# One-token decoder layer on one core: K and V loaded in four groups of eight heads instead of eight groups of four

## The chip, the cores and the metric

The kernel runs on one core of one Trainium2 chip. The metric is the device time of one launch in microseconds (us); lower is better. Times come in two kinds: the time of a whole launch, of which several were taken, and one launch under the profiler, whose span runs from its first to its last instruction.

## The reference

One decoder layer for one token. A is attention over a cache of 4096 positions with 32 heads of 128 elements, B is a gated MLP. All data is bf16.

```python
def _A_ref(x, k_cache, v_cache, wq, wo):            # x [1,1,640]; caches [1,32,4096,128]
    q = (x @ wq).reshape(B, Sq, Hq, Dh).transpose(0, 2, 1, 3)      # wq [640, 4096]
    scores = jnp.einsum("bhqd,bhkd->bhqk", q, k) * (Dh ** -0.5)
    p = _softmax(scores, axis=-1)
    o = jnp.einsum("bhqk,bhkd->bhqd", p, v)
    return o.transpose(0, 2, 1, 3).reshape(B, Sq, Hq * Dh) @ wo    # wo [4096, 640]

def _B_ref(x, w_gate, w_up, w_down):                # w_gate, w_up [640, 1728]; w_down [1728, 640]
    h = _gelu(x @ w_gate) * (x @ w_up)
    return h @ w_down

h  = x + _A_ref(_layernorm(x), A_k_cache, A_v_cache, A_wq, A_wo)
h2 = h + _B_ref(_layernorm(h), B_w_gate, B_w_up, B_w_down)
```

The two caches together are 67.1 MB, the weights 17.1 MB. Nothing is used twice.

## The kernel before

There is no scheduler: each operation is appended to its engine's list by hand (`V` VectorE, `A` ScalarE, `T` TensorE, `GP` GpSimd, `P.dma("sync", ...)` for the loads), with the earlier operations that it depends on; the lists are emitted in that order with semaphore waits. An engine therefore waits in order: what stands behind a waiting instruction waits too. All large loads are on SP's one queue.

**Buffers.** `slots` are three buffers of 34,560 B a partition. Each load of K or V for four heads (a group G of 0 to 7) fills 32 KB of one: 32 partitions a head, 128 positions a partition, 4 MB in all. `arena` holds wq and then wo. The order of the loads (`order`, L192) is wq, then K and V of groups 0 to 5 in turn, then K6, K7, V6, V7, then wo in two halves, then w_gate, w_up and w_down in pieces. A load into a slot waits for what last read it (`consumed`): for K that is the last product on VectorE, for V the last matmul.

**Scores** (`score_mult`, `score_sum`, L297 to L320). VectorE multiplies a chunk of 32 positions of every partition with the group's q, kept in `qb`, into one of four `prod` buffers (L301). TensorE folds the 128 elements of each position to 16 by eight matmuls with an identity matrix (the first at L311, the others through the helper at L29), and VectorE sums the 16 (L318) into `sc`. A group has four chunks.

**Softmax** (`head_max`, `exp_group`). The maximum over a partition's positions is taken (L323), scaled, made the maximum over a head's 32 partitions by a transpose of 32 by 32 blocks (L324 to L326), and used as the bias of exp on ScalarE (L329), which also sums. Then VectorE spreads the weights into a masked operand `p_bd` (L332), in which each partition's weight stands in its head's column alone.

**V** (`pv_group`, L337). 32 matmuls of 512 columns go four at a time to the four 32-row quarters of `po`, two banks of PSUM. `pick` (L359) masks what belongs together and `pick_sum` (L363 to L370) adds it up, in the last two groups by three additions. `head_sum` (L372) gathers the parts of a head, `normalize` divides, `spread` and `take` turn the result into columns `aP`, and `proj_part` multiplies them with wo. Behind it come the second layernorm, the gate (`glu`, L514), w_up, gelu, and w_down (`down`, L564).

**Order around the change.** VectorE gets, for each group, products and sums with the sum one chunk behind, the previous group's pick, the softmax, and then `p_bd`. V of group 6 is multiplied while K of group 7 is scored; V of group 7 follows its softmax. The last steps wait for weights that come behind the caches on the queue.

Of the kernel before, what the change touches and what calls it, by code (L numbers as in the profile page):

```python
# [11 lines left out]
D = 640  # L12
# [8 lines left out]
NG = 8  # L21
NSLOT = 3
# [88 lines left out]
def bass_sequential_preLN__gqa_block_cached__glu_gated_geglu__decode_kernel(nc, A_x, A_k_cache, A_v_cache, A_wq, A_wo, B_x, B_w_gate, B_w_up, B_w_down, out):  # L111
    sb = lambda name, shape, dt: nc.alloc_sbuf_tensor(name, shape, dt)
    SLOT = 10 * DF
    slots = [sb("slot%d" % i, [128, SLOT], BF16) for i in range(NSLOT)]
    arena = sb("arena", [128, 5 * 4096], BF16)
    prod = sb("prod", [128, 4, 32, DH], BF16)
    qb = sb("qb", [128, NG, DH], BF16)
    sc = sb("sc", [128, 2, 4, 32], FP32)
    mx = sb("mx", [128, NG], FP32)
    mxd = sb("mxd", [128, 2, 32], FP32)  # L120
    nb = sb("nb", [128, NG], FP32)
    p_t = sb("p_t", [128, 2, 128], BF16)
    p_bd = sb("p_bd", [128, 2, 128, 4], BF16)
    x_row = sb("x_row", [1, D], BF16)
    out_row = sb("out_row", [1, D], BF16)
    xx = sb("xx", [128, 10], FP32)
    ln = sb("ln", [128, 8], FP32)
    xlnB = sb("xlnB", [128, 5, 32], BF16)
    hT = sb("hT", [128, 10], FP32)
    hX = sb("hX", [128, 128, 5], FP32)  # L130
    hlnT = sb("hlnT", [128, 5], BF16)
    rz = sb("rz", [16, 2], FP32)
    po_m = sb("po_m", [128, 8, DH], FP32)
    po_r = sb("po_r", [128, 4, DH + 1], FP32)
    m8_t = sb("m8_t", [128, 8, 4, 4], FP32)
    m8 = sb("m8", [128, 8], FP32)
    hs_t = sb("hs_t", [128, 4, 32], FP32)
    hs = sb("hs", [128, 28], FP32)
    hb = sb("hb", [128, 28], FP32)
    aT = sb("aT", [16, 2, 128], BF16)  # L140
    aP = sb("aP", [128, 2, 16], BF16)
    sel = sb("sel", [16, 8, 128], BF16)
    A_hi = sb("A_hi", [128, D], BF16)
    A_lo = sb("A_lo", [128, D], BF16)
    rows = [sb("rows%d" % i, [128, 512], BF16) for i in range(2)]
# [10 lines left out]
    par_t = sb("par_t", [128, 2, 64], BF16)  # L156
    par = sb("par", [128, 2], FP32)
    one_bf = sb("one_bf", [1, 1], BF16)
    ones_f = sb("ones_f", [128, 128], FP32)
    mean_f = sb("mean_f", [128, 128], FP32)  # L160
    ones_b = sb("ones_b", [128, 1024], BF16)
    id_f = sb("id_f", [128, 128], FP32)
    id_b = sb("id_b", [128, 128], BF16)
    eps_t = sb("eps_t", [128, 1], FP32)
    zero_t = sb("zero_t", [128, 1], FP32)
    psum = lambda i, n=1: nc.alloc_psum_tensor("bank%d" % i, [128, 512 * n], FP32)
# [5 lines left out]
    ps_q = [bank[4], bank[7]]  # L172
# [4 lines left out]
    ps_p = bank[7]  # L177

    wo_sb = arena[:, :].rearrange("p (t i n) -> p t i n", t=2, i=16)
    view = lambda n: slots[n % NSLOT][:, 0:128 * DH].rearrange("p (g d) -> p g d", d=DH)  # L180

# [5 lines left out]


    A(lambda e: e.preload_act_table_set("natural_log_exp_and_others"))
    d_x = P.dma("scalar", x_row[:, :], A_x[0, :, :])  # L190
    d_wq = [P.dma("sync", arena[:, :], A_wq[:, :].rearrange("(p c) n -> p (c n)", c=5))]
    order = [(kind, G) for G in range(NG - 2) for kind in "KV"] + [(kind, G) for kind in "KV" for G in (NG - 2, NG - 1)]  # L192
    pos = {t: n for n, t in enumerate(order)}
    landed, consumed = {}, {}
    state = {"next": 0}
    d_wo = {}

    def wo_load(name, t, lo, hi):
        d_wo[name] = P.dma("sync", wo_sb[:, t, lo:hi, :],
                           A_wo[2048 * t:2048 * t + 2048, :].rearrange("(p i) n -> p i n", i=16)[:, lo:hi, :], qd)  # L200

    def issue(upto):
        while state["next"] < min(upto, len(order)):
            n = state["next"]
            kind, g = order[n]
            src = A_k_cache if kind == "K" else A_v_cache
            src = src[0, 4 * g:4 * g + 4, :, :].rearrange("h (p r) d -> (h p) (r d)", p=32)
            dst = slots[n % NSLOT][:, 0:128 * DH]
            landed[n] = P.dma("sync", dst, src, consumed[n - NSLOT] if n >= NSLOT else None)
            state["next"] = n + 1  # L210

    issue(NSLOT)


    c_one = V(lambda e: e.memset(one_bf[:, :], 1.0))
    c_ones = V(lambda e: e.memset(ones_f[:, :], 1.0))
    c_mean = V(lambda e: e.memset(mean_f[:, :], 1.0 / D))
    V(lambda e: e.memset(eps_t[:, :], EPS))
    c_eps = V(lambda e: e.memset(zero_t[:, :], 0.0))
    c_onesb = GP(lambda e: e.memset(ones_b[:, :], 1.0))  # L220
    c_idb = GP(lambda e: e.affine_select(id_b[:, :], ones_b[:, 0:128], pattern=[[1, 128]], compare_op=ALU.is_equal,
                                         fill=0.0, base=0, channel_multiplier=-1), c_onesb)
    c_idf = GP(lambda e: e.affine_select(id_f[:, :], ones_f[:, :], pattern=[[1, 128]], compare_op=ALU.is_equal,
                                         fill=0.0, base=0, channel_multiplier=-1), c_ones)
    c_sel = GP(lambda e: e.affine_select(sel[:, :, :], ones_b[0:16, :].rearrange("p (a b) -> p a b", a=8),
                                         pattern=[[-1, 8], [1, 128]], compare_op=ALU.is_equal,
                                         fill=0.0, base=0, channel_multiplier=-8), c_onesb)
    c_hz = GP(lambda e: e.memset(hs[:, :], 0.0))
    c_hb = GP(lambda e: e.memset(hb[:, :], 0.0))
    c_hb = GP(lambda e: e.affine_select(hb[:, 12:16], ones_f[:, 0:4], pattern=[[-32, 4]], compare_op=ALU.is_ge,  # L230
                                        fill=0.0, base=0, channel_multiplier=1), c_hb, c_ones)
    c_hb = GP(lambda e: e.affine_select(hb[:, 12:16], hb[:, 12:16], pattern=[[32, 4]], compare_op=ALU.is_ge,
                                        fill=0.0, base=31, channel_multiplier=-1), c_hb)
    c_hs = GP(lambda e: e.affine_select(hs_t[:, :, :], ones_f[:, :].rearrange("p (a b) -> p a b", a=4),
                                        pattern=[[-1, 4], [-4, 32]], compare_op=ALU.is_equal,
                                        fill=0.0, base=0, channel_multiplier=1), c_ones)
    c_s4 = GP(lambda e: e.affine_select(sel4[:, :], ones_b[:, 0:4], pattern=[[-32, 4]], compare_op=ALU.is_equal,
                                        fill=0.0, base=0, channel_multiplier=1), c_onesb)
    c_m8 = GP(lambda e: e.affine_select(m8_t[:, :, :, :], ones_f[:, :].rearrange("p (a b c) -> p a b c", a=8, b=4),
                                        pattern=[[-4, 8], [-32, 4], [-1, 4]], compare_op=ALU.is_equal,  # L240
                                        fill=0.0, base=0, channel_multiplier=1), c_ones)
    c_sel2 = GP(lambda e: e.affine_select(sel2[:, :, :], ones_b[0:64, 0:128].rearrange("p (a b) -> p a b", a=64),
                                          pattern=[[1, 64], [0, 2]], compare_op=ALU.is_equal,
                                          fill=0.0, base=0, channel_multiplier=-1), c_onesb)
    c_par = GP(lambda e: e.affine_select(par_t[:, :, :], ones_b[:, 0:128].rearrange("p (a b) -> p a b", a=2),
                                         pattern=[[-1, 2], [-2, 64]], compare_op=ALU.is_equal,
                                         fill=0.0, base=0, channel_multiplier=1), c_onesb)

    c_hs = V(lambda e: e.reduce_sum(hs[:, 12:16], hs_t[:, :, :], axis=AX.X), c_hs, c_hz)
    c_o4 = V(lambda e: e.reduce_max(ones4[:, :], sel4[:, :], axis=AX.X), c_s4)  # L250
    c_m8 = V(lambda e: e.reduce_sum(m8[:, :], m8_t[:, :, :, :].rearrange("p a b c -> p a (b c)"), axis=AX.X), c_m8)

    V(lambda e: e.reduce_sum(par[:, :], par_t[:, :, :], axis=AX.X), c_par)
# [9 lines left out]
    def layernorm(src, ev, out_fn):  # L263
# [8 lines left out]

    xl = layernorm(xx, xc, lambda e: e.tensor_scalar(
        xlnB[:, :, :], xx[:, 0:5].unsqueeze(2).to_broadcast([128, 5, 32]), ln[:, 0:1], ln[:, 4:5],
        ALU.subtract, ALU.mult))


    wq_j = arena[:, :].rearrange("p (c g j d) -> p c j g d", c=5, g=NG, j=4)

    def q_proj(e):  # L280
        for c in range(5):
            for hf in range(2):
                for j in range(4):
                    args = (ps_q[hf][32 * j:32 * j + 32, :], xlnB[:, c, :], wq_j[:, c, j, 4 * hf:4 * hf + 4, :])
                    if hf == 0:
                        i = e.matmul(*args, start=(c == 0), stop=(c == 4))  # L286
                    else:
                        i = matmul_again(nc, *args, c == 0, c == 4, (128, 32), (0, 32 * j))
        return i
    qd = T(q_proj, xl, *d_wq)  # L290
    qa = V(lambda e: e.tensor_copy(qb[:, 0:4, :].rearrange("p g d -> p (g d)"), ps_q[0][:, :]), qd)  # L291
    qc = A(lambda e: e.copy(qb[:, 4:8, :].rearrange("p g d -> p (g d)"), ps_q[1][:, :]), qd)


    folds, reds, exps, pbs, pvs, evs, hds = {}, {}, {}, {}, {}, {}, {}

    def score_mult(s):  # L297
        G, n = s // 4, pos[("K", s // 4)]
        kt = view(n)
        u = s % 4  # L300
        m = V(lambda e: e.tensor_tensor(  # L301
            out=prod[:, s % 4, :, :], in0=kt[:, 32 * u:32 * u + 32, :],
            in1=qb[:, G, :].unsqueeze(1).to_broadcast([128, 32, DH]), op=ALU.mult),
# [109 lines left out]
    def run(todo):  # L413
        while todo:
            todo.pop(0)()
# [200 lines left out]
```

## Time and profile before

| What | Value |
|---|---|
| Time before, median of 3 runs | 202.68 us (202.64 to 204.21) |
| Time of the profiled execution | 202.77 us |
| Its span | 201.5 us |
| Mean granted TensorE clock | 0.816 |
| Bytes read from HBM | 84.23 MB, 418 GB/s over the span |
| Busy: the load queue, of 16 transfer engines | 97.8% |
| Busy: VectorE / TensorE / ScalarE / GpSimd | 68% / 57% / 4% / 3% |

How to read it: in the lines of the profile PE is TensorE, PEld its weight loads, DVE VectorE, ACT ScalarE, POOL GpSimd and SP the engine that issues the loads. `L301` is a line of the kernel. A group's row gives its count, busy time and mean duration in ns, and after the second bar the idle time of the engine before it with what ended that time. Tile names come without their number: `slot` is any of the three buffers, `bank` any bank of PSUM. The span is 1.3 us shorter than the time of the same execution.

### The profile page before, as it was taken

The numbers are of one execution on the slowest core, as the hardware profiler recorded it, in microseconds if no ns is written. First come the engines' busy times: TensorE is split into PE (matmuls) and PEld (weight loads), VectorE is DVE, ScalarE is ACT, GpSimd is POOL, SyncE is SP. The second block draws the span as 40 slices with busy tenths as digits, with TensorE's granted clock in tenths as the row PEclk, the third lists the DMA queues.
The fourth block names the chain that finished last, engine by engine and source line by source line (L and its number), as shares of the span: only waits on it lengthen the run. The fifth ranks groups of instructions, "written<-read, shape, count | busy, mean of one in ns | idle before, by whom it ended". The sixth has DMA issues, their size and how long they took to land.

```text
span 201.5 us, 1482 instructions
## 1 busy us (share of the span) xinstructions
PE 115.2 (57%) x801; PEld 18.2 (9%) x397; DVE 136.3 (68%) x168; ACT 8.9 (4%) x27; POOL 5.1 (3%) x17
## 2 busy tenths in 40 slices
PE   0107058466628693686169717762874099374585
PEld 0101000010001000100010001000100001022323
DVE  1301088639991799699848985996799979853331
ACT  2101000000000000000000000000000000000111
POOL 7200000000000000000000000000000000000000
PEclk9999658969985579799976997996699669878555
DMA  9999999999999999999999999999999999999992
GB/s 342 431 398 455 449 416 416 423 436 462 439 416 423 418 423 455 455 423 416 423 413 442 449 449 423 416 423 429 442 442 442 423 419 407 439 407 439 414 403 94
DMA packets 4185, 84.31 MB, mean 418 GB/s; under 512 B 466, under 2 KB 980, under 8 KB 1492
## 3 DMA queue, kind: packets, MB, share of 16 engines
q1 hardware_dynamic: 4178, 84.23, 97.8%
q8 instruction: 4, 0.07, 0.1%
q14 instruction: 1, 0.01, 0.0%
q10 hardware_dynamic: 2, 0.00, 0.0%
HBM read 84.23 MB, written 0.00 MB: 418 GB/s over the span
## 4 chain that ended last, share of the span: by engine, by line
DMA 52%; DVE 28%; PE 16%; SPq 1%; issue 1%; ACT 0%
DMA slot<-in_A_k_cache_dram 40%; DVE prod L301 18%; DMA slot<-in_B_w_down_dram 13%; PE bank L29 11%; DVE sc L318 5%; DVE po_r L369 3%; PE bank L347 3%; PE bank L311 2%; SPq L60 1%; DVE p_bd L332 1%; DVE mx L323 1%; PE bank L564 0%; DVE mxd L325 0%; DVE mxd L324 0%; DVE nb L326 0%
## 5 line engine op out<-in xcount | busy, mean ns | idle before, releaser
L301 DVE TENSOR_TENSOR prod<-slot,qb 128x4096 bf16<-128x4096 bf16 x32 | 72.4, 2285 | 22.4 <-DMA slot<-in_A_k_cache_dram 22.4
L29 PE MATMUL bank<-prod,id_b 128*128 128x512 bf16 x224 | 60.8, 417 | 0.0
L347 PE MATMUL bank<-slot,p_bd 128*32 128x512 bf16 x128 | 19.0, 583 | 27.3 <-DVE p_bd L332 27.3
L311 PE MATMUL bank<-prod,id_b 128*128 128x512 bf16 x32 | 14.1, 439 | 35.4 <-DVE prod L301 35.4
L318 DVE TENSOR_REDUCE sc<-bank 128x32 f32<-128x512 f32 x32 | 22.0, 687 | 8.4 <-PE bank L29 8.2
L29 PE MATMUL bank<-slot,p_bd 128*32 128x512 bf16 x128 | 18.9, 580 | 0.0
L311 PEld LDWEIGHTS bank<-prod,id_b 128*128 128x128 bf16 x32 | 3.3, 103 | 89.4 <-DVE prod L301 89.2
L369 DVE TENSOR_REDUCE po_r<-po_m 128x128 f32<-128x1024 f32 x6 | 11.2, 1865 | 0.0
L359 DVE TENSOR_TENSOR po_m<-bank,m 128x1024 f32<-128x1024 f32 x8 | 9.7, 1215 | 2.2 <-PE bank L29 2.2
L329 ACT ACTIVATE p_t<-sc,nb 128x128 bf16<-128x128 f32 x8 | 3.2, 401 | 150.9 <-DVE nb L326 150.9
L347 PEld LDWEIGHTS bank<-slot,p_bd 128*32 128x32 bf16 x128 | 4.5, 130 | 54.4 <-DVE p_bd L332 40.0
L291 DVE CAST qb<-bank 128x512 bf16<-128x512 f32 x1 | 0.7, 690 | 9.3 <-PE bank L29 9.3
L286 PE MATMUL bank<-arena,xlnB 128*32 128x512 bf16 x20 | 2.8, 531 | 7.2 <-DMA arena<-in_A_wq_dram 7.2
L332 DVE TENSOR_TENSOR p_bd<-p_t,hb 128x512 bf16<-128x512 bf16 x8 | 5.5, 682 | 1.1 <-ACT p_t L329 1.1
L514 PE MATMUL bank<-slot,hlnT 128*1 128x512 bf16 (+1 forms) x40 | 4.6, 551 | 1.5 <-DVE hlnT L503 1.5
L376 PE MATMUL bank<-po_r,hs 128*16 128x128 f32 x16 | 3.7, 318 | 1.5 <-DVE po_r L367 1.5
L258 PE MATMUL bank<-one_bf,x_row 1*128 1x1 bf16 x5 | 0.4, 177 | 6.7 <-DMA x_row<-in_A_x_dram 6.7
L405 PE MATMUL bank<-arena,aP 128*1 128x320 bf16 x32 | 2.5, 298 | 1.0 <-DMA arena<-in_A_wo_dram 1.0
L564 PE MATMUL bank<-slot,hm 128*1 128x128 bf16 (+2 forms) x57 | 2.8, 323 | 0.1
L29 PE MATMUL bank<-arena,xlnB 128*32 128x512 bf16 x20 | 2.8, 528 | 0.0
L374 PEld LDWEIGHTS bank<-po_r,hb 128*16 128x16 f32 x16 | 2.0, 124 | 6.1 <-issue 5.8
L323 DVE TENSOR_REDUCE mx<-sc 128x1 f32<-128x128 f32 x8 | 2.3, 286 | 0.3
(94 smaller groups left out, 48.9 us busy)
## 6 DMA issues: line engine op xcount, KB each, us to landing
slot<-in_A_k_cache_dram SPq DMA_DIRECT2D x8, 4096.0 KB, 19.4
slot<-in_A_v_cache_dram SPq DMA_DIRECT2D x8, 4096.0 KB, 18.8
arena<-in_A_wq_dram SPq DMA_DIRECT2D x1, 5120.0 KB, 15.2
arena<-in_A_wo_dram SPq DMA_DIRECT2D x2, 2560.0 KB, 27.6
slot<-in_B_w_gate_dram SPq DMA_DIRECT2D x1, 2160.0 KB, 18.5
slot<-in_B_w_up_dram SPq DMA_DIRECT2D x1, 1296.0 KB, 21.1
slot<-in_B_w_down_dram SPq DMA_DIRECT2D x2, 640.0 KB, 24.4
slot<-in_B_w_up_dram SPq DMA_DIRECT2D x1, 864.0 KB, 22.7
```

The costliest lines, as they stand in the source:

```text
L29: return e.add_instruction(mybir.InstMatmult(name=nc.get_next_instruction_name(), engine=e.engine, start_tensor_calc=start, stop_tensor_ca ...
L301: m = V(lambda e: e.tensor_tensor(out=prod[:, s % 4, :, :], in0=kt[:, 32 * u:32 * u + 32, :], in1=qb[:, G, :].unsqueeze(1).to_broadcast([1 ...
L311: i = e.matmul(*args, start=True, stop=False)
L318: reds[s] = V(lambda e: e.reduce_sum(sc[:, (s // 4) % 2, s % 4, :], ps_f[s % 2][:, :].rearrange("p (g d) -> p g d", d=16), axis=AX.X), fol ...
L323: m = V(lambda e: e.reduce_max(mx[:, G:G + 1], sc[:, G % 2, :, :].rearrange("p u g -> p (u g)"), axis=AX.X), reds[4 * G + 3])
L329: exps[G] = A(lambda e: e.activation(p_t[:, G % 2, :], sc[:, G % 2, :, :].rearrange("p u g -> p (u g)"), ACTF.Exp, bias=nb[:, G:G + 1], sc ...
L332: pbs[G] = V(lambda e: e.tensor_tensor(out=p_bd[:, G % 2, :, :], in0=p_t[:, G % 2, :].unsqueeze(2).to_broadcast([128, 128, 4]), in1=hb[:, ...
L347: return e.matmul(*args, start=(c < 4), stop=(c >= 12))
L359: mks[G] = V(lambda e: e.tensor_tensor(out=po_m[:, :, :], in0=po[:, :].rearrange("p (b d) -> p b d", b=8), in1=m8[:, :].unsqueeze(2).to_br ...
L369: evs[G] = V(lambda e: e.reduce_sum(po_r[:, G % 4, 0:DH], po_m[:, :, :].rearrange("p b d -> p d b"), axis=AX.X), mks[G], hds.get(G - 4))
L376: hds[G] = T(lambda e: e.matmul(ps_a[0:16, at:at + DH], hs[:, 12 - 4 * g:28 - 4 * g], po_r[:, g, 0:DH], start=False, stop=(g == 3), skip_g ...
L514: i = e.matmul(po[32 * a:32 * a + 1, 512 * k:512 * k + n], hlnT[:, c:c + 1], w[:, c, 512 * a:512 * a + n], start=(c == 0), stop=(c == 4))
```

## The change

- K and V come in four groups of eight heads: 16 partitions a head, 256 positions a partition, rows of 64 KB, 8 MB a load. The last K alone comes in two halves, each half the positions of every partition. The order is wq, K0, V0, K1, V1, K2, V2, K3 (two halves), V3, wo, MLP weights.
- Three buffers of 64 KB a partition hold everything: buffer 2 first wq and some constants, then K1, V2 and wo; buffer 0 holds K0, V1, K3 and then all MLP weights; buffer 1 holds V0, K2, V3 and later a few small rows. `arena` and `prod` are gone.
- The product is written over K itself. A K buffer is free when the last fold on TensorE has read it, and no longer after the last product on VectorE.
- A group has eight chunks. The pick, head sum and, in group 2, the first normalize, spread and take stand between the chunks of the next group.
- The softmax works on 256 positions a partition. As two heads now share a 32-row block, `far` adds a large number in the other head's columns before the minimum.
- `p_bd` of a group is made in four parts (`PARTS`), each followed by its 16 matmuls on V: 64 of 512 columns a group, each with its own weights, into one bank of PSUM. Before there were 32 matmuls for half as many heads, two to a weight load.
- `pick` works on 512 columns instead of 1024, followed by two additions. `spread` is one matmul instead of eight, `take` a masked product and a sum instead of a copy.
- The identity is loaded on TensorE only where another operand was loaded since.
- The q projection writes one bank by 40 matmuls with masked columns (`xlnM`).

The diff, cut to its core:

```diff
-NG = 8
-NSLOT = 3
+NG = 4
+SLOT = 256 * DH
...
-    order = [(kind, G) for G in range(NG - 2) for kind in "KV"] + [(kind, G) for kind in "KV" for G in (NG - 2, NG - 1)]
...
+    order = [(kind, G) for G in range(NG) for kind in "KV"]
+    for n, t in enumerate(order):
+        home[t] = slots[n % 3][:, :]
...
+    def load(kind, G, half, *deps):
+        src = A_k_cache if kind == "K" else A_v_cache
+        src = src[0, 8 * G:8 * G + 8, :, :].rearrange("h (p r) d -> (h p) (r d)", p=16)
+        lo, hi = (0, SLOT) if half is None else (SLOT // 2 * half, SLOT // 2 * half + SLOT // 2)
+        landed[(kind, G, half)] = P.dma("sync", home[(kind, G)][:, lo:hi], src[:, lo:hi], *deps)
...
+    free2 = [qd, c_sel2, c_par, c_m4, c_m8, c_hs, c_idb]
...
+    def score_mult(G, c):
+        kt = tile("K", G)[:, 32 * c:32 * c + 32, :]
+        got = landed.get(("K", G, None)) or landed[("K", G, c // 4)]
+        m = V(lambda e: e.tensor_tensor(out=kt, in0=kt, in1=qb[:, G, :].unsqueeze(1).to_broadcast([128, 32, DH]), op=ALU.mult),
+              got, q1)
+        again, held[0] = held[0], True
...
+        folds[(G, c)] = T(fold, m, c_idb, reds.get((G, c - 2) if c >= 2 else (G - 1, c + 6)))
+        if c == 7:
+            done[("K", G)] = folds[(G, c)]
...
+        for n in range(PARTS):
+            lo, hi = 64 // PARTS * n, 64 // PARTS * (n + 1)
+            pbs[(G, n)] = pbs[G] = V(lambda e, lo=lo, hi=hi: e.tensor_tensor(
+                out=p_bd[:, lo:hi, :].rearrange("p c (a r) -> p c a r", a=8),
+                in0=p_t[:, 4 * lo:4 * hi].rearrange("p (c r) -> p c r", r=4).unsqueeze(2).to_broadcast([128, hi - lo, 8, 4]),
+                in1=hbx[:, :, :].unsqueeze(1).to_broadcast([128, hi - lo, 8, 4]), op=ALU.mult),
+                exps[G], pvs.get(G - 1), c_hx)
+
+    def attend(G):
+        vt = tile("V", G)
+        for n in range(PARTS):
+            def pv(e, n=n):
+                for c in range(64 // PARTS * n, 64 // PARTS * (n + 1)):
+                    a = 32 * (c % 4)
+                    i = e.matmul(po[a:a + 32, 0:512], p_bd[:, c, :], vt[:, 4 * c:4 * c + 4, :],
+                                 start=(c < 4), stop=(c >= 60))
+                return i
+            pvs[G] = done[("V", G)] = other(pv, pbs[(G, n)], landed[("V", G, None)], mks.get(G - 1))
...
+    PARTS = 4
+    for G in range(NG):
+        for c in range(8):
+            score_mult(G, c)
+            if c >= 1:
+                score_sum(G, c - 1)
+            if c == 1 and G:
+                pick(G - 1)
+            if c == 3 and G:
+                head_sum(G - 1)
+            if c == 4 and G == 2:
+                normalize(0)
+            if c == 5 and G == 2:
+                spread(0)
+            if c == 6 and G == 2:
+                take(0)
+        score_sum(G, 7)
+        softmax(G)
+        if G == 0:
+            load("K", 1, None, *free2)
+            load("V", 1, None, done[("K", 0)])
+        attend(G)
+        if G == 0:
+            load("K", 2, None, done[("V", 0)])
+        if G == 1:
+            load("V", 2, None, done[("K", 1)])
+            for h in range(2):
+                load("K", 3, h, done[("V", 1)])
+        if G == 2:
+            load("V", 3, None, done[("K", 2)])
...
+    d_wo = [P.dma("sync", wo_sb[:, t, :, :], A_wo[2048 * t:2048 * t + 2048, :].rearrange("(p i) n -> p i n", i=16), done[("V", 2)])
+            for t in range(2)]
+    free = done[("K", 3)]
```

More of the change, by code (lines that the diff above doesn't have):

```diff
@@ L112, in bass_sequential_preLN__gqa_block_cached__glu_gated_geglu__decode_kernel @@
     sb = lambda name, shape, dt: nc.alloc_sbuf_tensor(name, shape, dt)
[L113 to L116, printed above, removed]
+    slots = [sb("slot%d" % i, [128, SLOT], BF16) for i in range(3)]
+    mix = sb("mix", [128, 1024], FP32)
     qb = sb("qb", [128, NG, DH], BF16)
-    sc = sb("sc", [128, 2, 4, 32], FP32)
+    sc = sb("sc", [128, 256], FP32)
     mx = sb("mx", [128, NG], FP32)
     mxd = sb("mxd", [128, 2, 32], FP32)
+    neg = sb("neg", [128, 32], FP32)
+    far = sb("far", [128, 2, 16], FP32)
+    odd = sb("odd", [128, 2], FP32)
     nb = sb("nb", [128, NG], FP32)
[L122 to L125, printed above, removed]
+    p_t = sb("p_t", [128, 256], BF16)
     xx = sb("xx", [128, 10], FP32)
     ln = sb("ln", [128, 8], FP32)
-    xlnB = sb("xlnB", [128, 5, 32], BF16)
+    xlnM = sb("xlnM", [128, 352], BF16)
     hT = sb("hT", [128, 10], FP32)
-    hX = sb("hX", [128, 128, 5], FP32)
     hlnT = sb("hlnT", [128, 5], BF16)
     rz = sb("rz", [16, 2], FP32)
[L133 to L139, printed above, removed]
+    po_r = sb("po_r", [128, 2, DH + 1], FP32)
+    m4 = sb("m4", [128, 4], FP32)
+    hs = sb("hs", [128, 24], FP32)
+    hb = sb("hb", [128, 24], FP32)
+    hbx = sb("hbx", [128, 8, 4], BF16)
     aT = sb("aT", [16, 2, 128], BF16)
     aP = sb("aP", [128, 2, 16], BF16)
[L142 to L145, printed above, removed]
+    sel = sb("sel", [16, 16, 8], BF16)
+    m8 = sb("m8", [128, 8], FP32)
+    aM = sb("aM", [128, 8, 16], FP32)
     sel4 = sb("sel4", [128, 4], BF16)
@@ L165, in bass_sequential_preLN__gqa_block_cached__glu_gated_geglu__decode_kernel, with __init__, take @@
     zero_t = sb("zero_t", [128, 1], FP32)
+    p_bd = mix[:, :].bitcast(BF16).rearrange("p (c x) -> p c x", x=32)
+    po_m = mix[:, 0:4 * DH].rearrange("p (b d) -> p b d", b=4)
+    hX = mix[:, 0:128 * 5].rearrange("p (a c) -> p a c", c=5)
+    class Cut:
+        def __init__(self, slot, at):
+            self.slot, self.at = slot, at
+        def take(self, n, parts=128):
+            ap = self.slot[0:parts, self.at:self.at + n]
+            self.at += n
+            return ap
+    first_t = Cut(slots[2], 5 * 4096)
+    ones_b = first_t.take(128)
+    m4_t = first_t.take(128).rearrange("p (a b) -> p a b", a=4)
+    hs_t = first_t.take(128).rearrange("p (a b c) -> p a b c", a=8, b=4)
+    m8_t = first_t.take(128).rearrange("p (a b) -> p a b", a=8)
+    par_t = first_t.take(128).rearrange("p (a b) -> p a b", a=2)
+    x_row = first_t.take(D, 1)
+    last_t = Cut(slots[1], 0)
+    A_hi, A_lo = last_t.take(D), last_t.take(D)
+    rows = [last_t.take(512) for _ in range(2)]
+    out_row = last_t.take(D, 1)
     psum = lambda i, n=1: nc.alloc_psum_tensor("bank%d" % i, [128, 512 * n], FP32)
@@ L198, in wo_load @@
[L198 to L210, printed above, removed]
@@ L280, in q_proj @@
     def q_proj(e):
         for c in range(5):
-            for hf in range(2):
+            for s in range(2):
                 for j in range(4):
[L284 to L288, printed above, removed]
-        return i
@@ L290, in bass_sequential_preLN__gqa_block_cached__glu_gated_geglu__decode_kernel @@
[L290 to L303, printed above, removed]
-            landed[n], qa, qc, folds.get(s - 4))
-        consumed[n] = m
+                    i = e.matmul(ps_q[32 * j:32 * j + 32, :], xlnM[:, 160 * s + 32 * c:160 * s + 32 * c + 32], wq_j[:, c, 2 * j + s, :, :],
+                                 start=(c == 0 and s == 0), stop=(c == 4 and s == 1))
@@ L337, in pv_group @@
-    def pv_group(G):
-        n = pos[("V", G)]
-        vt = view(n)
-        def pv_mm(e, c, half, load):
-            a = 32 * (c % 4)
-            args = (po[a:a + 32, 512 * half:512 * half + 512],
-                    p_bd[:, G % 2, 8 * c:8 * c + 8, :].rearrange("p g j -> p (g j)"),
-                    vt[:, 8 * c + 4 * half:8 * c + 4 * half + 4, :])
-            if load:
-                return e.matmul(*args, start=(c < 4), stop=(c >= 12))
-            return matmul_again(nc, *args, c < 4, c >= 12, (128, 32), (0, a))
-        def pv(e):
-            for c4 in range(4):
-                for half in range(2):
-                    for c in range(4 * c4, 4 * c4 + 4):
-                        i = pv_mm(e, c, half, half == 0)
-            return i
-        pvs[G] = consumed[n] = T(pv, pbs[G], landed[n], mks.get(G - 1))
+        exps[G] = A(lambda e: e.activation(p_t[:, :], sc[:, :], ACTF.Exp, bias=nb[:, G:G + 1], scale=INV_SQRT_DH,
+                                           accum_out=po_r[:, G % 2, DH:DH + 1]), nbs[G], pbs.get(G - 1), hds.get(G - 2))
@@ L391, in spread, with take @@
-        spr[t] = T(fn, z4s[t], c_sel)
-    def take(t):
-        aPs[t] = V(lambda e: e.tensor_copy(aP[:, t, :], ps_z[:, 32:48]), spr[t])
+        spr[t] = other(lambda e: e.matmul(ps_z[:, 32:160], sel[:, :, :].rearrange("p a b -> p (a b)"), aT[:, t, :], start=True, stop=True),
+                       z4s[t], c_sel)
+    def take(t):
+        m = V(lambda e: e.tensor_tensor(out=aM[:, :, :], in0=ps_z[:, 32:160].rearrange("p (q i) -> p q i", q=8),
+                                        in1=m8[:, :].unsqueeze(2).to_broadcast([128, 8, 16]), op=ALU.mult), spr[t], c_m8)
+        def fn(e):
+            with nc.allow_low_precision(reason="one of the eight terms is not zero"):
+                return e.reduce_sum(aP[:, t, :], aM[:, :, :].rearrange("p q i -> p i q"), axis=AX.X)
+        aPs[t] = V(fn, m)
@@ L409, in proj_part @@
         return T(fn, *ws)
-    first, later = [], []
-    def run(todo):
-        while todo:
-            todo.pop(0)()
-    def scores(G):
-        for i in range(4):
-            score_mult(4 * G + i)
-            if i >= 1:
-                score_sum(4 * G + i - 1)
-            if i == 1 and G == NG - 1:
-                attend(G - 1)
-        run(first)
-        score_sum(4 * G + 3)
-        head_max(G)
-        if G < NG - 1:
-            run(later)
-        exp_group(G)
-        run(later)
-        issue(pos[("K", G)] + 1 + NSLOT)
@@ L433, in bass_sequential_preLN__gqa_block_cached__glu_gated_geglu__decode_kernel @@
-    headed = []
-    def attend(G):
-        pv_group(G)
-        while len(headed) in evs:
-            head_sum(len(headed))
-            headed.append(G)
-        if G == NG - 1:
-            return
-        first.append(lambda: pick(G))
-        later.append(lambda: pick_sum(G))
-        if G == 4:
-            later.append(lambda: normalize(0))
-        if G == 5:
-            spread(0)
-            later.append(lambda: take(0))
-    for kind, G in order:
-        if kind == "K":
-            scores(G)
-            continue
-        if G != NG - 2:
-            attend(G)
-        issue(pos[("V", G)] + 1 + NSLOT)
```

191 lines of the change are left out of this document (87 added, 104 removed).

## The prediction

> **What bounds the kernel now.** I read the profile's page first, for the share of each resource.
>
> ```profile
> span 201.5 us, 1482 instructions
> PE 115.2 (57%) x801; PEld 18.2 (9%) x397; DVE 136.3 (68%) x168; ACT 8.9 (4%) x27; POOL 5.1 (3%) x17
> DMA packets 4185, 84.31 MB, mean 418 GB/s; under 512 B 466, under 2 KB 980, under 8 KB 1492
> q1 hardware_dynamic: 4178, 84.23, 97.8%
> DMA 52%; DVE 28%; PE 16%; SPq 1%; issue 1%; ACT 0%
> L301 DVE TENSOR_TENSOR prod<-slot,qb 128x4096 bf16<-128x4096 bf16 x32 | 72.4, 2285 | 22.4 <-DMA slot<-in_A_k_cache_dram 22.4
> L369 DVE TENSOR_REDUCE po_r<-po_m 128x128 f32<-128x1024 f32 x6 | 11.2, 1865 | 0.0
> L332 DVE TENSOR_TENSOR p_bd<-p_t,hb 128x512 bf16<-128x512 bf16 x8 | 5.5, 682 | 1.1 <-ACT p_t L329 1.1
> ```
>
> The transfer engines work 97.8% of the span and VectorE 68%. The chain gives DVE 28% only because each K load was released by an earlier piece of work; that does not make DVE the bound. The windows decide it (us, busy by engine, granted clock, DMA share, GB/s):
>
> ```profile
> core 0: us, PE busy (x) PEld busy (x) DVE busy (x) ACT busy (x) POOL busy (x), PEclk, DMA share, GB/s
> 24.90:103.50 78.60, 49.34 (x264) 4.78 (x89) 60.40 (x58) 1.98 (x8) 0.00 (x0) 0.81 1.00 431
> 103.50:142.40 38.90, 23.64 (x136) 2.45 (x47) 32.01 (x32) 0.99 (x4) 0.00 (x0) 0.85 1.01 433
> 171.60:181.60 10.00, 5.50 (x74) 1.60 (x40) 6.80 (x14) 0.49 (x2) 0.00 (x0) 0.83 0.99 420
> ```
>
> No gap: the share is 1.00 and the rate 431 to 433 GB/s from the first K load on. The chain of waits dates the arrivals (start, us, what):
>
> ```profile
> 24.96 2.30 DVE prod L301
> 27.31 0.61 PE bank L311
> 27.92 3.00 PE bank L29 x7
> ...
> 33.83 0.60 DVE sc L318
> 34.43 2.21 DVE prod L301
> ...
> 37.08 1.52 PE bank L29 x7
> ...
> 85.83 17.71 DMA slot<-in_A_k_cache_dram
> ...
> 124.10 18.29 DMA slot<-in_A_k_cache_dram
> ```
>
> K of group 4 lands at 85.83 + 17.71 = 103.54 and K of group 6, four loads later, at 142.39: 38.85 / 4 = 9.71 us for each 4 MB, or 432 GB/s. So the bytes set the end. The change matters only if it alters the bytes, the rate, the queue's feeding, or the short chain behind the last arrivals. That chain stands in the timeline (start, us, engine, line, out<-in; in brackets idle time):
>
> ```profile
> 166.34 0.40 PE L347 MATMUL bank<-slot,p_bd 128*32 128x512 bf16 x4
> 166.56 0.39 PE L29 MATMUL bank<-slot,p_bd 128*32 128x512 bf16 x4
> 170.26 0.33 SPq L60 DMA_DIRECT2D slot<-in_B_w_down_dram  x1
> 172.96 0.29 DVE L323 TENSOR_REDUCE mx<-sc 128x1 f32<-128x128 f32 x1
> 173.96 0.40 ACT L329 ACTIVATE p_t<-sc,nb 128x128 bf16<-128x128 f32 x1 [17.24 <-DVE nb L326]
> 175.64 0.64 PE L29 MATMUL bank<-slot,p_bd 128*32 128x512 bf16 x4
> 176.06 0.64 PE L347 MATMUL bank<-slot,p_bd 128*32 128x512 bf16 x4
> 178.72 1.23 DVE L359 TENSOR_TENSOR po_m<-bank,m 128x1024 f32<-128x1024 f32 x1 [2.15 <-PE bank L29]
> 179.98 0.69 DVE L365 TENSOR_TENSOR po_m<-po_m 128x512 f32<-128x512 f32 x1
> 181.16 0.29 DVE L367 TENSOR_TENSOR po_r<-po_m 128x128 f32<-128x128 f32 x1
> 182.92 0.17 DVE L394 CAST aP<-bank 128x16 bf16<-128x16 f32 x1 [0.45 <-PE bank L389]
> 183.90 0.31 PE L405 MATMUL bank<-arena,aP 128*1 128x320 bf16 x4 [1.02 <-DMA arena<-in_A_wo_dram]
> 189.57 1.87 PE L514 MATMUL bank<-slot,hlnT 128*1 128x512 bf16 x17 [1.49 <-DVE hlnT L503]
> 194.36 0.10 PEld L514 LDWEIGHTS bank<-slot,hlnT 128*1 128x1 bf16 x8 [0.78 <-DMA slot<-in_B_w_up_dram]
> 198.68 0.25 PEld L564 LDWEIGHTS bank<-slot,hm 128*1 128x1 bf16 x12 [0.48 <-DMA slot<-in_B_w_down_dram]
> ```
>
> The last pieces of w_down are still waited for at 198.68. The attention result aP is ready at 183.09 and waits 0.8 us for wo; later w_up is waited for by 0.78 and w_down by 0.48. Of a delay of aP, 0.8 + 0.78 + 0.48 = about 2.1 us is covered.
>
> **The change, part by part.**
>
> *Bytes and order.* Each cache byte, wq, wo and MLP byte is still loaded once, on the same queue. With 8 MB loads the arrivals are those of before, taken by pairs. From K at 24.95 and 9.71 a step: K0 34.7, V0 about 54, K1 74, V1 93, K2 113.2, V2 132.7, the two halves of K3 142.4 and 152.1 (as K6 and K7 before), V3 171.5, wo 183.9. Cost: 0.
>
> *Fewer, longer rows.* A transfer engine gets 8 rows of each load: before 16 x 8 = 128 cache rows, after 7 x 8 + 2 x 8 = 72, so 56 fewer. No row of the trace prices one; I bound it. The 97.8% of 16 engines is 3153 us for 4178 packets and 84.23 MB; a 32 KB row at 433 GB/s takes 1.211 us. If a packet costs a plus its bytes, those two give a = 0.025 us, an upper bound, since the slow first packets are in it. The lower bound is nothing (a 64 KB row might be sent as two). 56 x 0 to 0.025 is 0 to 1.4 us saved; I take 0.5, nearer to zero because of the first packets. Seven fewer issues on SP (0.33 each) are hidden: the queue holds loads already.
>
> The Trainium skill (SBUF — State Buffer, The DMA setup-cost knee) gives a transfer about 2 us fixed beside its bytes; by it seven fewer loads would save some 14 us. The 9.71 us from load to load says that queued loads do not pay it, so I do not use it.
>
> *Feeding the queue.* Every load waits on SP, in order, for the last user of its buffer, and K's buffer is now held until the last fold on PE instead of the last product. Four chunks take 24.96 to 38.60 from arrival to the end of the last fold, so eight take 13.6 + 4 x 2.81 (2.21 product, 0.60 sum) = 24.9 us; pick, normalize and take inside add up to 2.4. After it: softmax about 2.6 (last sum 0.69, a maximum over 256 near 0.42, three small operations near 0.2, exp about 0.7 with its sum read out, gaps), the first mask part 0.68, then 64 matmuls: 16 rounds of four at 0.42 (clock at half) or 0.22, 3.5 to 6.9 us. V1 is issued when K0 is done, at 59.6, with K1 still arriving until 74; K2 after V0, about 70 against 93; V2 after K1, about 101 against 113; K3 about 111 against 132.7; V3 after K2, 140.5 against 152.1; wo about 150 against 171.5; the MLP weights after K3's last fold, 171.1 against wo's 183.9 (170.26 before). The smallest cover is 11.6 us. Cost 0; without that cover each microsecond late is one of span, for all queued behind.
>
> *VectorE.* Products in place: 32 of the same shape, priced at the old 2.28. The in-place additions at L365 and L367 take 0.69 and 0.29 for 512 and 128 elements, one element a cycle, so in place is not dear there; for the bf16 product no row shows it, and its upper bound is the p_bd rate of L332 (512 in 0.68), twice as slow or worse. I take equal, as the shape and operands are. Pick works on half the elements (0.69 for 1.21), and the sum of 1.87 becomes two additions (about 0.45 + 0.29): off the bound, worth nothing. p_bd grows from 8 to 16 of 0.68: 5.5 us more, spread over idle DVE, but some in front of K3.
>
> *The tail.* K2's folds end at 113.2 + 24.9 + 2.4 = 140.5, softmax 143.1, four mask parts 145.6. So K3 starts 3.2 us after its first half is there. Eight products (17.6) and seven sums (4.2), pick 1.4 and a wait for PE of about 0.8 (it still multiplies V2): the last fold ends near 171.1, first mask part 174.4. V3 has landed by then. After an idle stretch PE runs at half clock for about 3.6 us (the first fold, 27.31 to 30.92), which is 8.6 rounds, then the other 7.4 at full: 5.2 us, 179.6, bounds 177.9 to 181.3. Pick and two additions take 0.69 + 0.45 + 0.29 and gaps, 1.5; from the end of L367 to the end of aP's copy were 1.64 (181.45 to 183.09), with one small operation more and seven matmuls less I take 1.8: aP at 182.9, bounds 181.2 to 184.6. Before it was 183.09. Even the late bound is 1.5 us, inside the 2.1 covered (1.6 when the stream ends 0.5 sooner). Cost 0.
>
> *Start.* Other constants and the projection in one bank lie before K0's arrival. Before, the first product only waited for K at 24.96; now K0 is whole at 34.7, so the same preparation has 9.7 us more: 0.
>
> *Sum.* The profiled execution: 202.77 us, span 201.5. Minus 0.5: 202.3; the median of the runs shown, 202.68, is 0.1 under the profiled one, so **202.2 us**, no change by the bound of 1% (about what a measurement of this kernel can tell from no change).
>
> **Rivals.**
>
> 1. *The tail becomes the bound* (slower). All of the last eight heads now pass K3, softmax and V3 in one pass, where before V6 went through while K7 was scored. For it: K3 starts late by 3.2 us and everything after is serial. Against: it ends level with before by my sum. It decides once aP is later than about 185; from there each microsecond counts. If PE stays at half clock, the p_bd parts hold up PE, and K2 ends 2 us later than summed, aP comes near 187 and the time is about 204.5; up to 206.
>
> 2. *The long rows are read more slowly* (slower). For it: rates in the windows do differ, 420 to 433. Against: 431 to 433 wherever 32 KB rows run alone. 67.1 MB of cache at 420 instead of 432 take 4.5 us more: 206.7. The Trainium skill (DMA: Bandwidth & Descriptors, Latency and other measured facts) lists copies slowed by large power-of-two row pitches, 207 GB/s at 512 KiB against 214 when padded. By it, taken as 3% of the cache, an estimate of 5 us. No run here shows a pitch above 32 KB.
>
> 3. *The in-place product runs at half speed* (slower). A chunk then takes about 4.2 + 0.6, a group of eight 38.4 plus about 9 of the rest against 38.85 of supply; DVE becomes the bound and the time goes to 230 or more. Nothing in the trace speaks for it.
>
> 4. *Fewer rows and loads save more* (faster). At the upper price, 1.4 us, and with as much again for the seven completions saved or a shorter lag of the last engine, 200.3.
>
> 5. *The rows are cut back to 32 KB pieces*, so that this part does nothing: 202.7, inside the forecast.
>
> **How the numbers follow.** Forecast with rival 5: 0.68, with its own range 201.3 to 203.2. Rival 1: 0.12, rival 2: 0.08, rival 3 or a queue that runs dry after all: 0.04. Rival 4: 0.08. So slower by over 1% (above 204.7) has 0.24, counting rival 1 whole, faster by over 1% (below 200.7) 0.08, within 0.68. The range 201.0 to 205.5 takes the forecast and most of rival 1 and leaves out 4, 3 and the dear end of 2.
>
> **What would show it.** Right: 430 GB/s or more and share 1.00 in every window up to 171; K rows of the chain landing at about 35, 74, 113; no idle DMA slice; products of 2.28 us; aP between 181 and 185 with a wait for wo or w_up behind it. Wrong: a DMA slice below 9 tenths before 195, an SP row that issues a load after the one before it has landed, products above 2.4 us, cache windows under 425 GB/s, or a last down-projection that does not wait for w_down.

## The result and the profile after

| | Before | After |
|---|---|---|
| Median | 202.70 us (22 runs, 202.54 to 204.21) | 202.24 us (22 runs, 201.93 to 202.43) |
| Ratio after to before | | 0.9968, 95% interval 0.9958 to 0.9979 |
| Profiled execution, span | 202.77 us, 201.5 us | 202.1 us, 200.9 us |

The change gains 0.46 us, 0.3%. That is clear of the noise and far below 1%. The forecast was 202.2.

From the page of the changed kernel:

```profile
span 200.9 us, 1518 instructions
PE 110.0 (55%) x771; PEld 17.7 (9%) x491; DVE 118.5 (59%) x160; ACT 6.8 (3%) x18; POOL 4.2 (2%) x19
DMA packets 3178, 84.32 MB, mean 420 GB/s; under 512 B 354, under 2 KB 868, under 8 KB 1380
q1 hardware_dynamic: 3170, 84.23, 97.8%
L315 DVE TENSOR_TENSOR slot<-slot,qb 128x4096 bf16<-128x4096 bf16 x32 | 72.7, 2282 | 32.7 <-DMA slot<-in_A_k_cache_dram 32.7
L346 DVE TENSOR_TENSOR mix<-p_t,hbx 128x512 bf16<-128x512 bf16 x16 | 5.7, 420 | 2.7 <-ACT p_t L342 2.7
```

VectorE lost 17.8 us of work (136.3 to 118.5), and the time moved by half a microsecond. The bytes and the 97.8% are the same. What differs on the load queue is the packet count: 1008 fewer. Of these 896 are cache rows (a 64 KB row is one packet). The other 112 are small packets, sixteen for each of the seven loads fewer: those under 512 B fell from 466 to 354.

The chain of waits of the changed kernel (start, us, what) dates the arrivals and the ends of the folds:

```profile
0.45 34.28 DMA slot<-in_A_k_cache_dram
...
34.76 2.30 DVE slot L315
...
57.68 1.90 PE bank L29 x8
...
69.18 43.34 DMA slot<-in_A_k_cache_dram
...
112.54 2.30 DVE slot L315
...
138.66 1.90 PE bank L29 x8
...
143.64 5.25 PE bank L358 x64
...
169.09 1.90 PE bank L29 x8
...
173.75 24.28 DMA slot<-in_B_w_down_dram
```

K0 is there at 34.73 and K2 at 112.51, four loads of 8 MB later: 77.78 / 4 = 19.45 us each, against 2 x 9.71 before. The last folds of K0, K2 and K3 end at 59.6, 140.6 and 171.0.

SP's part of the timeline, the issues of the loads:

```profile
59.60 0.33 SPq L60 DMA_DIRECT2D slot<-in_A_v_cache_dram  x1
69.18 0.33 SPq L60 DMA_DIRECT2D slot<-in_A_k_cache_dram  x1
100.07 0.33 SPq L60 DMA_DIRECT2D slot<-in_A_v_cache_dram  x1
108.20 1.20 SPq L60 DMA_DIRECT2D slot<-in_A_k_cache_dram  x2
140.58 0.33 SPq L60 DMA_DIRECT2D slot<-in_A_v_cache_dram  x1
148.94 0.80 SPq L60 DMA_DIRECT2D slot<-in_A_wo_dram  x2
171.00 0.33 SPq L60 DMA_DIRECT2D slot<-in_B_w_down_dram  x1
```

Each stands at the end of the fold or of the V matmuls that frees its buffer. K2, whose load is issued at 69.18, lands at 112.51; in between lie V1 and K2 itself, so the queue was never empty.

Two kinds of line seem to speak against that, the busy share of the transfer engines in 40 slices and the windows over the later loads (the last columns are the DMA share and GB/s):

```profile
DMA  9999999999999999999999999799999998999993
103.50:142.40 38.90, 24.02 (x133) 2.30 (x64) 26.60 (x29) 0.00 (x0) 0.00 (x0) 0.84 0.98 423
152.10:170.50 18.40, 11.58 (x53) 0.25 (x5) 17.50 (x14) 0.00 (x0) 0.00 (x0) 1.00 0.93 402
112.50:142.40 29.90, 19.36 (x69) 0.55 (x8) 26.03 (x27) 0.00 (x0) 0.00 (x0) 0.83 1.00 434
```

The 7 stands at 126 to 131 us, and yet the window from 112.5 to 142.4, which contains it, shows 434 GB/s. The views count each packet whole where it starts, and a 64 KB row is one packet of 2.42 us on each of 16 engines; where the edge of a slice or a window falls among these starts, up to 1 MB is counted on the wrong side. If each packet of the trace is counted by the part of its time that lies in the window, the two windows have 433 and 432 GB/s at a share of 1.00, and no stretch of 1 us between 2 and 186 us has a share below 0.99.

The timeline of the tail (in brackets the idle time of the engine before, and what ended it):

```profile
143.16 1.43 DVE L346 TENSOR_TENSOR mix<-p_t,hbx 128x512 bf16<-128x512 bf16 x4 [0.67 <-ACT p_t L342]
144.51 4.49 DVE L315 TENSOR_TENSOR slot<-slot,qb 128x4096 bf16<-128x4096 bf16 x2
150.76 0.69 DVE L332 TENSOR_REDUCE sc<-bank 128x32 f32<-128x512 f32 x1 [1.77 <-PE bank L29]
174.06 5.32 PE L358 MATMUL bank<-slot,mix 128*32 128x512 bf16 x64 [3.08 <-DVE mix L346]
182.57 0.37 DVE L391 TENSOR_REDUCE aP<-aM 128x16 bf16<-128x128 f32 x1
183.26 0.31 PE L403 MATMUL bank<-slot,aP 128*1 128x320 bf16 x4 [1.05 <-DMA slot<-in_A_wo_dram]
193.74 0.10 PEld L490 LDWEIGHTS bank<-slot,hlnT 128*1 128x1 bf16 x8 [0.79 <-DMA slot<-in_B_w_up_dram]
196.34 1.06 PE L540 MATMUL bank<-slot,hm 128*1 128x128 bf16 x37
198.07 1.17 PE L540 MATMUL bank<-slot,hm 128*1 128x128 bf16 x20 [0.67 <-DMA slot<-in_B_w_down_dram]
```

The three waits of the tail are still there: wo, w_up, w_down. Each ends 0.6 us earlier than before (183.90, 194.36 and 198.68 then). The whole shift is in the arrivals.

### The profile page after: what moved, and what is told of

Its sections match the earlier page's. It is cut to its first block, busy times and chain, and to the rows that moved or that the text cites. A ratio compares the mean times of both kernels' runs of the same rounds, so it can differ in the third digit from the quotient of the medians.

```text
span 200.9 us, 1518 instructions
## 1 busy us (share of the span) xinstructions
PE 110.0 (55%) x771; PEld 17.7 (9%) x491; DVE 118.5 (59%) x160; ACT 6.8 (3%) x18; POOL 4.2 (2%) x19
## 3 DMA queue, kind: packets, MB, share of 16 engines
q1 hardware_dynamic: 3170, 84.23, 97.8%
## 4 chain that ended last, share of the span: by engine, by line
DMA 51%; DVE 30%; PE 16%; SPq 1%; issue 1%; ACT 0%
DMA slot<-in_A_k_cache_dram 39%; DVE slot L315 21%; DMA slot<-in_B_w_down_dram 12%; PE bank L29 8%; DVE sc L332 6%; PE bank L358 6%; SPq L60 1%; PE bank L323 1%; DVE mix L364 1%; PE bank L540 1%; DVE mix L346 0%; DVE mix L367 0%; DVE mx L337 0%; ACT p_t L342 0%; DVE po_r L368 0%
## 5 line engine op out<-in xcount | busy, mean ns | idle before, releaser
L315 DVE TENSOR_TENSOR slot<-slot,qb 128x4096 bf16<-128x4096 bf16 x32 | 72.7, 2282 | 32.7 <-DMA slot<-in_A_k_cache_dram 32.7
L29 PE MATMUL bank<-slot,id_b 128*128 128x512 bf16 x248 | 66.2, 419 | 21.7 <-DVE slot L315 21.7
L358 PE MATMUL bank<-slot,mix 128*32 128x512 bf16 x256 | 22.1, 521 | 12.3 <-DVE mix L346 12.3
L323 PE MATMUL bank<-slot,id_b 128*128 128x512 bf16 x8 | 3.8, 471 | 33.5 <-DVE slot L315 33.5
L358 PEld LDWEIGHTS bank<-slot,mix 128*32 128x32 bf16 x256 | 8.3, 126 | 72.1 <-DVE mix L346 61.3
L297 PE MATMUL bank<-slot,xlnM 128*32 128x512 bf16 x40 | 4.5, 630 | 7.3 <-DMA slot<-in_A_wq_dram 7.3
L342 ACT ACTIVATE p_t<-sc,nb 128x256 bf16<-128x256 f32 x4 | 2.0, 507 | 161.8 <-DVE nb L341 161.8
L346 DVE TENSOR_TENSOR mix<-p_t,hbx 128x512 bf16<-128x512 bf16 x16 | 5.7, 420 | 2.7 <-ACT p_t L342 2.7
L364 DVE TENSOR_TENSOR mix<-bank,m 128x512 f32<-128x512 f32 x4 | 2.7, 684 | 4.4 <-PE bank L358 4.4
L403 PE MATMUL bank<-slot,aP 128*1 128x320 bf16 x32 | 2.2, 299 | 1.0 <-DMA slot<-in_A_wo_dram 1.0
L29 PE MATMUL bank<-slot,aP 128*1 128x320 bf16 x32 | 2.2, 299 | 0.0
L374 PE MATMUL bank<-po_r,hs 128*16 128x128 f32 x8 | 1.5, 272 | 0.5 <-DVE po_r L368 0.5
```

The costliest lines, as they stand in the source:

```text
L29: return e.add_instruction(mybir.InstMatmult(name=nc.get_next_instruction_name(), engine=e.engine, start_tensor_calc=start, stop_tensor_ca ...
L297: i = e.matmul(ps_q[32 * j:32 * j + 32, :], xlnM[:, 160 * s + 32 * c:160 * s + 32 * c + 32], wq_j[:, c, 2 * j + s, :, :], start=(c == 0 an ...
L315: m = V(lambda e: e.tensor_tensor(out=kt, in0=kt, in1=qb[:, G, :].unsqueeze(1).to_broadcast([128, 32, DH]), op=ALU.mult), got, q1)
L323: i = e.matmul(*args, start=True, stop=False)
L346: pbs[(G, n)] = pbs[G] = V(lambda e, lo=lo, hi=hi: e.tensor_tensor(out=p_bd[:, lo:hi, :].rearrange("p c (a r) -> p c a r", a=8), in0=p_t[: ...
L358: i = e.matmul(po[a:a + 32, 0:512], p_bd[:, c, :], vt[:, 4 * c:4 * c + 4, :], start=(c < 4), stop=(c >= 60))
```

## Experiments

Three theories for the 0.46 us stood against each other: R, the rows saved; L, the loads saved; T, something in the tail or in the other work. Four kernels on one chip tell them apart. The comparison was with 202.71 us for the kernel before (27 runs).

**The changed kernel again**, as the level.

> The changed kernel itself, as the level for the three kernels beside it. All theories: 202.2 us, about 0.3% under the kernel before. What has to be explained is 0.46 us. Theory R (rows): a transfer engine gets 56 fewer rows, each of which costs some 8 ns beside its bytes. Theory L (loads): nine loads instead of sixteen, each with a cost of its own. Theory T (tail or other work): the gain is not in the transfers, but in what stands behind the last arrivals.

Measured: 202.17 us (202.07 to 202.41), ratio 0.9976 (0.9967 to 0.9985).

**Rows of 32 KB in the same nine loads.**

```diff
+PIECES = 2
+PIECE = SLOT // PIECES
+STEP = PIECE + 32
...
-    slots = [sb("slot%d" % i, [128, SLOT], BF16) for i in range(3)]
+    slots = [sb("slot%d" % i, [128, PIECES * STEP], BF16) for i in range(3)]
...
+    def part(kind, G, at, n):
+        lo = at * DH + at * DH // PIECE * 32
...
+        dst = home[(kind, G)].rearrange("p (s x) -> p s x", s=PIECES)[:, lo:hi, 0:PIECE]
+        landed[(kind, G, half)] = P.dma("sync", dst, src.rearrange("p (s x) -> p s x", s=PIECES)[:, lo:hi, :], *deps)
```

> The changed kernel with a gap of 64 bytes in the middle of each buffer row, so that a 64 KB row arrives as two rows of 32 KB; the nine loads, their order and all computation stay. R: 56 rows per transfer engine come back, +0.45 us, 202.7 us. L and T: 202.2 us, no change.

Measured: 202.60 us (202.44 to 203.25), ratio to before 0.9993 (0.9972 to 1.0013). That is 0.43 us over the changed kernel, and each of the 11 runs lies above each of the changed kernel's 11: the gain is nearly gone, with nothing changed but the rows and the gaps that cut them. From its page:

```profile
q1 hardware_dynamic: 4066, 84.23, 97.9%
```

**Rows of 8 KB in the same nine loads** (`PIECES = 8`).

> The same with seven gaps, rows of 8 KB, nine loads still. R: 512 cache rows per transfer engine instead of 72; 440 more at 8 to 9 ns are +3.5 to +4.0 us, 205.7 to 206.2 us (at the upper bound of the prediction, 25 ns, it would be 213 us). L and T: 202.2 us.

Measured: 205.52 us (205.19 to 205.71), ratio to before 1.0141 (1.0127 to 1.0155). From its page, and its window over the cache loads, with the window of the changed kernel behind it (the last columns are the DMA share and GB/s):

```profile
q1 hardware_dynamic: 10210, 84.23, 98.4%
```

```profile
20.00:140.00 120.00, 59.08 (x325) 4.69 (x143) 75.62 (x73) 1.20 (x4) 0.00 (x0) 0.83 1.01 425
```

```profile
20.00:140.00 120.00, 65.47 (x328) 5.19 (x143) 76.72 (x74) 1.20 (x4) 0.00 (x0) 0.80 1.00 432
```

The share stays at 1: the engines are never idle, they carry less. A row costs about the same at both steps: 56 more rows an engine, +0.43 us, 7.7 ns each; 440 more, +3.35 us, 7.6 ns each. The small step is uncertain by some 0.2 us; the large one is the better price. The packets of the traces say the same: in the median a row of 64 KB takes 2.418 us, two of 32 KB take 2.426 and eight of 8 KB 2.472, which is 8 ns for each further row.

**Sixteen loads with rows of 32 KB.**

```diff
-        landed[(kind, G, half)] = P.dma("sync", home[(kind, G)][:, lo:hi], src[:, lo:hi], *deps)
+        for h in range(2) if half is None else (half,):
+            lo, hi = SLOT // 2 * h, SLOT // 2 * h + SLOT // 2
+            landed[(kind, G, h)] = P.dma("sync", home[(kind, G)][:, lo:hi], src[:, lo:hi], *deps)
...
-              got, q1)
+              first, got, q1)
...
```

> The changed kernel with every cache load issued as two loads of half the columns, 16 loads of 4 MB with rows of 32 KB; VectorE and TensorE wait for both halves, buffers, order and computation stay. R: as with rows of 32 KB in nine loads, 202.7 us. L: at 2 us of fixed cost for each of seven more loads 216 us; at a cost of completion only, below 0.1 us each, 202.7 us at most together with the rows. T: 202.2 us.

Measured: 202.71 us (202.54 to 202.87), the same as before (0.9996, 0.9983 to 1.0009). Beside the nine loads with the same rows it is +0.11 us, 16 ns for each of seven loads if the difference is real; the two ranges overlap. So rows and loads together return the whole gain, although all the new computation stays. R holds and T falls: the rows are most of the gain, and L, if it is there at all, is about a quarter of it. The Trainium skill (SBUF — State Buffer, The DMA setup-cost knee) gives every transfer a roughly fixed cost of about 2 us; by it seven more loads would cost 14 us, an estimate. These loads, which wait in a queue, do not pay it: seven more cost 0.11 us. The slowing by large row pitches that the Trainium skill lists from 512 KiB on, for copies within HBM (DMA: Bandwidth & Descriptors, Latency and other measured facts), does not show here at 64 KB: this kernel reads every 32 KB row at that pitch, in the time of the kernel before.

Four more tell how far the two covers of the prediction reach, the queue's and the tail's. The kernel before took 202.65 us beside them (17 runs). The changed kernel was not run beside these four; they are compared with its 202.17 us from above, where the kernel before took 202.71.

**V3 loaded late.**

```diff
             score_mult(G, c)
+            if c == 3 and G == 3:
+                load("V", 3, None, folds[(3, 3)])
...
-        if G == 2:
-            load("V", 3, None, done[("K", 2)])
```

> The changed kernel, with the load of V3 held until TensorE has folded the fourth chunk of K3 instead of the last of K2: issued near 159.9 instead of 140.6 us, while the second half of K3 lands at 151.3. Theory F (feeding): 10.7 us of cover are used up, the transfer engines run dry for some 9.5 us and the first byte takes about 1 us more; everything behind shifts: 212 to 213 us. Rival: the queue's later work or the tail takes the gap up, 202.2 to 204 us.

Measured: 214.77 us (two runs, 214.66 and 214.89), ratio 1.0588 (1.0546 to 1.0630). Its issue, and its windows in the gap, over the first row of V3 on every engine, and over the seven rows behind it (DMA share and GB/s last):

```profile
160.61 0.33 SPq L60 DMA_DIRECT2D slot<-in_A_v_cache_dram  x1
```

```profile
150.00:161.50 11.50, 8.31 (x33) 0.16 (x4) 9.62 (x9) 0.00 (x0) 0.00 (x0) 0.85 0.00 0
161.50:164.50 3.00, 1.90 (x8) 0.10 (x1) 3.00 (x4) 0.00 (x0) 0.00 (x0) 1.00 1.01 350
164.50:181.40 16.90, 5.66 (x24) 0.00 (x0) 9.46 (x15) 0.60 (x2) 0.00 (x0) 0.83 1.01 434
```

F holds in kind: a queue that runs dry is paid in full, nothing later takes it up. It cost 12.6 us over the changed kernel, some 2 more than summed, and lies above the 212 to 213 forecast. The packets of the trace account for it. The engines' last rows of K3 end between 149.3 and 150.9 us, 149.8 in the mean; the first rows of V3 start between 161.6 and 162.5, 161.8 in the mean. That is 12.0 us without work. The first row then takes 3.02 us instead of 2.42, another 0.6. The expectation had counted from the landing of K3's second half, 151.3, when the engines had been out of rows for 1.5 us in the mean; the issue was 0.7 us later than reckoned, and the slow first row was not in it.

**The last K in one load.**

```diff
-            for h in range(2):
-                load("K", 3, h, done[("V", 1)])
+            load("K", 3, None, done[("V", 1)])
```

> The changed kernel with the last K in one load of 64 KB rows, not in two halves. Its first product starts at 151.2 instead of 144.5 us; the wait of 1.8 us for TensorE goes, so the last fold is about 5.4 us later, with the first fold at half clock up to 6.7. Theory C (cover): behind aP 2.0 us are covered (0.3 before wo, 0.8 before w_up, 0.9 before w_down); the rest counts, +3.4 us, 205.6 us (204.8 to 207). Theory B (bytes alone set the end): 8 rows per transfer engine fewer, 202.1 us.

Measured: 206.50 us (205.96 to 207.10), ratio to before 1.0181 (1.0147 to 1.0214): 4.3 us over the changed kernel, in C's range and above its 205.6. B falls. From its timeline:

```profile
151.56 4.49 DVE L315 TENSOR_TENSOR slot<-slot,qb 128x4096 bf16<-128x4096 bf16 x2 [6.66 <-DMA slot<-in_A_k_cache_dram]
189.21 0.37 DVE L391 TENSOR_REDUCE aP<-aM 128x16 bf16<-128x128 f32 x1
201.60 1.33 PE L539 MATMUL bank<-slot,hm 128*1 128x128 bf16 x57
```

VectorE idles 6.66 us before the first product. aP is ready at 189.58, 6.64 later than with the halves. No wait for wo, w_up or w_down is left: the 57 matmuls of the down-projection run in one piece. This part of the change, the two halves, is worth 4.3 us to the new kernel.

**Six and sixteen idle operations in front of the last mask.** The diff is that of six; the second kernel has 16 in their place.

```diff
+    idle = sb("idle", [128, 16], FP32)
...
+        for k in range(6 if G == 3 else 0):
+            V(lambda e, k=k: e.reduce_max(idle[:, k:k + 1], sc[:, :], axis=AX.X), nbs[G])
```

> The changed kernel with six unneeded maxima over the scores (0.42 us each) on VectorE between the last softmax and its mask; 0.67 of the 2.5 us lie under exp, so aP comes 1.9 us later. C: inside the 2.0 us that are covered, 202.2 us (at most 202.4). Rival D (only the wait for wo covers): +1.5 us, 203.7 us.

> The same with sixteen of them, aP 6.05 us later. C: 4.0 us over the cover, 206.2 us. D: +5.7 us, 207.9 us. B (bytes alone): 202.2 us.

Measured: 202.32 us with six (201.96 to 203.05), ratio to before 0.9983 (0.9966 to 0.9999); 205.16 us with sixteen (203.62 to 206.11), ratio 1.0129 (1.0093 to 1.0166). From the timeline with six, then with sixteen:

```profile
173.24 2.05 DVE L346 TENSOR_REDUCE idle<-sc 128x1 f32<-128x256 f32 x6
183.78 0.37 DVE L394 TENSOR_REDUCE aP<-aM 128x16 bf16<-128x128 f32 x1
```

```profile
171.58 5.32 DVE L346 TENSOR_REDUCE idle<-sc 128x1 f32<-128x256 f32 x16
186.79 0.37 DVE L394 TENSOR_REDUCE aP<-aM 128x16 bf16<-128x128 f32 x1
199.20 1.33 PE L543 MATMUL bank<-slot,hm 128*1 128x128 bf16 x57
```

My delay was mis-sized: back to back such a maximum takes 0.34 us, not 0.42. Only the profiled execution of each shows its aP. With six, aP came at 184.15, 1.2 us later than in the changed kernel, and the profiled execution took 202.00 us against 202.1: covered, and D, which has only the 0.3 us before wo, falls. With sixteen, aP came at 187.16, 4.2 us later, and that execution, the fastest of its four, took 203.62: 1.5 us paid, 2.7 covered. B, which has no place for a loss, falls again. The profiled execution with the last K whole says the same: aP 6.6 us later, 206.01 against 202.1, 2.7 covered.

## Why the prediction was right, point by point

- **The bound.** The bytes set the end, and 17.8 us less of VectorE work did not move it. Right, and shown from the other side: the same computation with the old rows and loads takes the old time.
- **Fewer, longer rows.** Forecast 0.5 us with bounds of 0 and 1.4. Measured 0.43 for the rows and perhaps 0.1 for the loads, which the prediction had put at nothing. The step "nearer to zero because of the first packets" was right: 7.6 ns a row against the 9 taken and the bound of 25. But the 0.5 was chosen between the bounds and came from no row of the trace; that it fell within 0.1 us is in part luck.
- **Feeding.** Issues forecast at 59.6, about 70, 101, 111, 140.5, 150 and 171.1; they stand at 59.60, 69.18, 100.07, 108.20, 140.58, 148.94 and 171.00. K3's is early because K1's folds ended 0.9 us sooner and V1 was multiplied in 5.0 us, not the 6.9 of half clock throughout. The smallest cover, forecast at 11.6 us, was 10.7 by the landing of K3's second half, and 9.2 by the time at which the engines run out of rows (149.8 in the kernel with the late V3). That kernel also shows that the cover was needed, and what its loss costs.
- **VectorE.** The in-place product takes 2282 ns against 2285: rival 3 is gone. The price of the mask was wrong: 0.68 taken, 0.42 measured for one and 1.43 for four in a row, so that sixteen cost what eight had cost (5.7 us busy against 5.5), where the prediction had 5.5 more. I took the old row as one of bf16 operands; its second operand, `hb`, is fp32, and the new one, `hbx`, is bf16. That this is the cause was not run by itself. The error was hidden: it brought K3's first product to 144.5 instead of 145.6, and the longer wait for PE (1.77 instead of 0.8) took most of it back. That the two errors nearly cancel is luck.
- **The tail.** Forecast aP at 182.9, measured 182.94, with its steps: last fold 171.1 (171.0), matmuls on V from 174.4 to 179.6 (174.06 to 179.38). Rival 1 did not come. The cover was forecast at 2.1 us; 2.7 were measured. In the delayed tails the 57 down matmuls run together in 1.33 us; in the changed kernel 20 of them stand behind the wait for w_down and take 1.17 alone. The sum of the three waits did not count that. With it the cover comes out: 0.3 before wo, 0.8 before w_up, and 1.6 at the end, as 57 matmuls begun at 196.34 would end at 197.67 and not at 199.24; 2.7 in all.
- **Rivals 2, 4 and 5.** The long rows are not read more slowly, the saving is not 1.4 us, and a 64 KB row is not cut: 896 fewer packets.
- **The signs.** Two of the signs named for "wrong" did appear: slices below 9 tenths (a 7 and an 8), and cache windows under 425 GB/s (423 and 402). They were badly chosen, as these views count long packets where they start; taken packet by packet the stream ran at 432 to 433 GB/s with no gap.

None of these versions beats the changed kernel. VectorE's freed time lies under the transfers, and still longer rows were not tried.

## What to carry to other kernels

Where the transfer engines are at a share of 1 from end to end, price a change by three things: bytes, rows, and whether the queue ever runs dry. Here 7.6 ns a row was nearly the whole effect, while 18 us of VectorE work counted for nothing. Before buffers are made larger and released later, list the issue of each load against the end of the load before it; the smallest distance is the margin, and beyond it the loss is paid in full. The margin is somewhat shorter than that list says, as the engines run out of rows before the load is reported as landed (149.8 against 151.3 here). Where packets are long, do not read a dip in a short slice as a gap before a wider window shows it too. And a large last load needs cutting: its halves kept 4.3 us out of the tail.

## What the runs showed that I had not expected

- A queue that has run dry starts with a slow first row: the sixteen first rows of the late V3 took 2.5 to 3.4 us, 3.02 in the mean, against 2.42 for those behind them, which ran at 434 GB/s.
- When the computation sets the end, the executions spread: 203.62 to 206.11 us with sixteen idle operations, against 202.07 to 202.41 for the changed kernel beside the row experiments. Up to K3's last fold the three kernels do the same, and yet that fold ended at 169.64, 171.00 and 171.30 in the profiles with sixteen, none and six idle operations; the granted clock in the middle of it differs too (0.89, 0.81 and 0.81 from 143.2 to 152). While the transfers set the end, this spread does not reach the time.
